# Opening of a scan-and-gate kernel: a bank for each turned tile, three groups for the first tokens, warming products on a cleared tile and in the gaps

## The chip, the cores and the metric

The kernel runs on one core of one Trainium2 chip. A core has five engines that run on their own and wait for each other by semaphores: TensorE (PE, matrix products; PEld is its weight load), VectorE (DVE), ScalarE (ACT), GpSimd (POOL) and SyncE (SP, which here issues nearly all DMAs). Products are summed in PSUM, which has eight banks; DVE and ACT read them out. The metric is the device time of one launch in microseconds (us); the median of some runs counts.

## What is computed

Tokens x (2048 of 448 numbers, bf16) are normalized, and then go two ways: through a diagonal complex recurrence (A) and through a gated product of three matrices (B). The results are multiplied.

```python
xn = _layernorm(x)
# A: Bu = xn @ B_bar.T;  h[t] = Lam_bar * h[t-1] + Bu[t];  s = 2 * real(h @ C.T) + xn * Dskip
s = _A_ref(xn, ...)
# B: g = xn @ w_gate (448 x 1792); u = xn @ w_up; h = sigmoid(g) * u; h @ w_down (1792 x 448)
g = silu(_B_ref(xn, ...))
return x + s * g
```

## The kernel before

**Tiling.** The 2048 tokens are cut into four chunks of 512 (TC), a chunk into four tiles of 128 tokens. Features of xn lie on partitions after a turn (transposition), as four blocks of 128 (KT = 4, the middle ones overlapping so that 64 rows of w_gate and 64 of w_up, the "tails", share one weight tile wt). The 1792 columns of w_gate and w_up are 14 groups of 128 (ft). A group has a gate sum g_ps and an up sum u_ps, each 128 x 512 in fp32, which is one bank each. One sum takes three whole products (128 rows) and one tail (64 rows).

**Order.** The order on every engine is the written order: `keep_order` at the end ties each instruction to the one before it on its engine. So a waiting instruction holds up all behind it on its engine.

**The opening (chunk 0, lines 928 to 1026)** differs from the rest. Input tiles come one by one; weights for groups 0 to 3 (512 columns) come behind them on SP's queue, then those for groups 4 to 9. PE first runs `warm(22)`: 128 x 128 products of the identity tile `ident`, which POOL builds with a memset and an affine select (L136, L137), into a bank that nobody reads. Then `turn_twice` turns the three vectors log_dt, Lambda_im, Lambda_re (tile `rows`), and `warm(5)` follows. For the first two tiles DVE takes the statistics (`ln_stats`, L214 and L215), ACT the inverse deviation (`ln_inv`, L249 and L250), DVE normalizes (`ln_norm`, L272), PE turns the tile with four 128 x 128 products (`ln_turn`, L286) into the PSUM tile `tps`, and DVE copies it out to xnT (`ln_out`, L289). For the third tile the sums come from ACT, for the fourth from DVE, and POOL takes the power (L244). A `warm(4)` stands behind the first two turns.

`tps` is one tile of one bank with a place for an even and an odd token tile (`tps[:, j % 2, ...]`). A copy out of it and a turn into it are therefore kept apart: each pair of copies stands behind both turns.

**Groups of the first tokens.** With the first two tiles (256 tokens, HC) in xnT, PE starts groups 0 to 3: `gu_wholes` (L713) runs whole products of a group's gate (which = 0) or up sum (1) over a stretch of tokens; `gu_half` (L706) runs a tail. The order is: gate 0, 1, 2, 3; up 0, 1; third turn; up 2; fourth turn; tails of groups 0 to 2 for the first and then the second 256 tokens; tails of group 3; then whole products of groups 0 to 2 over the second 256 tokens, and group 3's rest. All sums are complete only then, and `gu_out` (ACT, tanh, L719) and `up_copy` (DVE, L999) empty them. Between these, `emit_frac` and `emit_abs` (DVE, L429 and L435) and `emit_sin` and `emit_cos` (ACT, L440 and L443) build the angle tables of the recurrence.

**Behind the opening** two sums run side by side on the upper and lower 64 rows of PE (`beside_each`, products at L514), from group 4 on: `group` emits pairs of units (gate and up of a group, or `bu`, the input of the recurrence, whose weights bT come by DMA transposes at L294). A bank is free for a new sum when ACT or DVE has emptied its old one. ACT empties them with sigmoid and copy (L752).

**Banks.** All PSUM tiles share one tag with eight places. In the opening these are warm_ps, tp_v (the vectors), tps and the eight of four groups (`gus`), so that some groups take a bank over from warm_ps, tp_v or tps.

Of the kernel before, what the change touches and what calls it, by code (L numbers as in the profile page):

```python
# [11 lines left out]
BF16 = mybir.dt.bfloat16  # L12
# [5 lines left out]
D = 448  # L18
F = 1792
P = 128  # L20
TC = 512
HC = TC // 2
NCH = S_TOK // TC
TPC = TC // P
KT = 4
# [6 lines left out]
K_ROWS = (0, 128, 192, 320)  # L32
# [19 lines left out]
def two_runs(ap: bass.AP, step: int, n: int) -> bass.AP:  # L52
    return bass.AP(tensor=ap.tensor, offset=ap.offset, ap=[*ap.ap[:-1], [step, 2], [1, n]])
# [18 lines left out]
def kernel(  # L72
# [18 lines left out]
    pe, act, dve, pool, sync = nc.tensor, nc.scalar, nc.vector, nc.gpsimd, nc.sync  # L91
    w = ctx.enter_context(tc.tile_pool(name="w", bufs=1))
# [5 lines left out]
    ps = ctx.enter_context(tc.tile_pool(name="ps", bufs=2, space=bass.MemoryType.PSUM))  # L98
# [9 lines left out]
    xnT = [w.tile([P, KT, TC], BF16, name=f"xnT{c}") for c in range(3)]  # L108
# [10 lines left out]
    ident = w.tile([P, P], BF16, name="ident")  # L119
# [53 lines left out]
        sync.dma_start_transpose(out=ctr[nm][:, :, kt * CP:(kt + 1) * CP], in_=raw[nm][0:CP, kt, :])  # L173


    hpi = w.tile([P, 1], FP32, name="hpi")
    dve.memset(hpi[:], HALF_PI)
    sgn = w.tile([P, 1], FP32, name="sgn")
# [14 lines left out]

    warm_ps = ps.tile([P, P], FP32, name="warm_ps", tag="bank", bufs=8)

    def warm(n):
        for _ in range(n):
            pe.matmul(warm_ps[:], lhsT=ident[:], rhs=ident[:], start=True, stop=True)  # L198

    def turn_twice(o, src, n):  # L200

        for kt in range(3):
            pe.transpose(o[:, kt, 0:n], src[:, kt * P:(kt + 1) * P], ident[0:n, 0:n])
        pe.transpose(o[:, 3, 0:n], src[:, D - P:D], ident[0:n, 0:n])
        pe.transpose(o[0:64, 3, 0:n], src[:, 384:D], ident[0:n, 0:n])
# [10 lines left out]


    sums = w.tile([P, NT, 2], FP32, name="sums")

    junk = w.tile([P, D], BF16, name="junk")  # L220

    def ln_sum(t):
        c, j = divmod(t, TPC)
# [40 lines left out]
    def ln_norm(c, j):  # L264
        t = c * TPC + j
        xb, src = xn[c % 3][:, j, :], x_t[c][:, j, :]
        if c == 0:
            xb = xb[:, 0:D]
        else:
            xb, src = two_runs(xb, 2 * P, 2 * P), two_runs(src, 192, 2 * P)  # L270
        if c < 2:
            dve.tensor_scalar(out=xb, in0=src, scalar1=mv[:, t, 0:1], scalar2=rsd[:, t, :], op0=ALU.subtract,  # L272
                              op1=ALU.mult)
        else:
            act.activation(xb, src, ACT.Identity, bias=nmr[:, t, :], scale=rsd[:, t, :])
# [4 lines left out]
    def ln_turn(c, j):  # L280
        xb, cols = xn[c % 3], slice(j * P, (j + 1) * P)
        if c > 0:
            sync.dma_start_transpose(out=xnT[c][:, 0:KT, cols], in_=xb[:, j, :])
            return
        for kt in range(KT):
            pe.transpose(tps[:, j % 2, kt, :], xb[:, j, K_ROWS[kt]:K_ROWS[kt] + P], ident[:])  # L286

    def ln_out(j):
        dve.tensor_copy(out=xnT[0][:, :, j * P:(j + 1) * P], in_=tps[:, j % 2, :, :])  # L289

# [40 lines left out]
    def emit_steps():  # L333
        kq, nf, anf = col("kq", 2 * KT), col("nf", 2 * KT), col("anf", 2 * KT)
        tu = col("tu", 2 * KT)
        pool.tensor_copy(out=tu[:, 0:KT], in_=K["turn"][:])
        pool.tensor_single_scalar(out=tu[:, KT:2 * KT], in_=K["theta"][:], scalar=float(TC) / TWO_PI, op=ALU.mult)
        pool.tensor_single_scalar(out=kq[:], in_=tu[:], scalar=MAGIC, op=ALU.add)
        pool.tensor_single_scalar(out=kq[:], in_=kq[:], scalar=-MAGIC, op=ALU.add)
        pool.tensor_tensor(out=nf[:], in0=kq[:], in1=tu[:], op=ALU.subtract)  # L340
        K.update(nf=nf, anf=anf)
# [85 lines left out]
    def emit_frac(pt):  # L427
        f = sp.tile([P, HC], FP32, name="frac", tag="wv")
        dve.scalar_tensor_tensor(out=f[:], in0=iota_f[:], scalar=K["turn"][:, pt:pt + 1], in1=K[pt][:],  # L429
                                 op0=ALU.mult, op1=ALU.subtract)  # L430
        K[pt] = f

    def emit_abs(pt):
        af = sp.tile([P, HC], FP32, name="afrac", tag="td")
        dve.tensor_single_scalar(out=af[:].bitcast(I32), in_=K[pt][:].bitcast(I32), scalar=0x7FFFFFFF,  # L435
                                 op=ALU.bitwise_and)
        K[pt, 1] = af
# [62 lines left out]
    def bank(name, n=TC):  # L500
        return ps.tile([P, n], FP32, name=name, tag="bank", bufs=8)
# [27 lines left out]
    class Unit:  # L529

        ft = None
# [172 lines left out]
    def gu_half(c, ft, i, t, first, n0, n1):  # L704
        p0, kt = ((0, 1), (64, 2))[i]
        pe.matmul(t[:, n0:n1], lhsT=wt[p0:p0 + 64, ft * P:(ft + 1) * P], rhs=xnT[c][p0:p0 + 64, kt, n0:n1],  # L706
                  start=first, stop=not first)

    def gu_wholes(c, ft, gt, ut, first, n0=0, n1=TC, which=(0, 1)):
        f0, f1 = ft * P, (ft + 1) * P  # L710
        for t, wm, kts in [((gt, wg, GATE_K), (ut, wu, UP_K))[i] for i in which]:
            for k, kt in enumerate(kts):
                pe.matmul(t[:, n0:n1], lhsT=wm[:, k, f0:f1], rhs=xnT[c][:, kt, n0:n1],  # L713
                          start=(first and k == 0), stop=(not first and k == 2))
# [194 lines left out]
    def ln_plan(c):  # L909
        own, t0, n = c - 1, c * TPC, 2 if c == 2 else 0  # L910
        for k in range(n):
            at(0, 11 + k, 0.8, lambda t=t0 + k: ln_stats(t))
        t1, m = t0 + n, TPC - n
        steps = [lambda t=t: ln_sum(t) for t in range(t1, t1 + m)] + [lambda: ln_mean(t1, m)]
        steps += [lambda t=t: ln_square(t) for t in range(t1, t1 + m)]
        for k, f in enumerate(steps):
            at(own - 1, (10, 10, 11, 11, 12)[k] if c == 2 else "out%d" % min(k // 2, 3), 0.0, f)
        if n:
            at(0, 12, 0.17, lambda: ln_var(t0, n))
        then = (0, 13) if c == 2 else (own, 1)  # L920
        at(*then, 0.17, lambda: ln_var(t1, m, True))
        at(*then, 0.17, lambda: ln_minus(c))
        at(own, "down0", 0.0, lambda: (ln_pow(t0, TPC), ln_scale(c)))
        for j in range(TPC):
            at(own, "down0", 0.0, lambda j=j: ln_norm(c, j))
        at(own, "down0", 0.0, lambda: [ln_turn(c, j) for j in range(TPC)])

    dummy = w.tile([P, 1], FP32, name="dummy")
    act.add_instruction(mybir.InstLoadActFuncSet(name=nc.get_next_instruction_name(), act_func_set_id=LN_AND_EXP,
                                                 ins=[], outs=[]))  # L930
    warm(22)
    turn_twice(tp_v, rows, 3)
    tps = ps.tile([P, 2, KT, P], BF16, name="tp_x", tag="bank", bufs=8)
    gus = [(bank("g_ps"), bank("u_ps")) for _ in range(4)]
    warm(5)

    ln_stats(0)
# [6 lines left out]
    ln_sum(2)  # L944
    ln_norm(0, 0)
    ln_turn(0, 0)
    ln_norm(0, 1)
    ln_turn(0, 1)
    warm(4)
    ln_out(0)  # L950
    ln_out(1)
    ln_mean(2, 1)
    ln_square(2)
# [5 lines left out]
    act.activation(K["r"][:], K["arg"][:], ACT.Exp)  # L959
    act.activation(dummy[:], hpi[:], ACT.Silu)  # L960

    for ft in range(4):
        gu_wholes(0, ft, *gus[ft], True, 0, HC, (0,))
    for ft in range(2):
        gu_wholes(0, ft, *gus[ft], True, 0, HC, (1,))
    ln_norm(0, 2)
    ln_turn(0, 2)
    emit_frac(0)
    gu_wholes(0, 2, *gus[2], True, 0, HC, (1,))
    ln_norm(0, 3)  # L970
    ln_turn(0, 3)
    ln_out(2)
    emit_abs(0)
    ln_out(3)
    for pt in (1, 3, 2):
        emit_frac(pt)
        emit_abs(pt)
    for n0 in (0, HC):
        for ft in range(3):
            for i in range(2):  # L980
                gu_half(0, ft, i, gus[ft][i], n0 > 0, n0, n0 + HC)
    gu_half(0, 3, 0, gus[3][0], False, 0, HC)
    gu_half(0, 3, 1, gus[3][1], True, 0, TC)
    gu_half(0, 3, 0, gus[3][0], True, HC, TC)
    for ft in range(3):
        gu_wholes(0, ft, *gus[ft], False, HC, TC)
    gu_wholes(0, 3, *gus[3], False, HC, TC, (0,))
    gu_wholes(0, 3, *gus[3], False, 0, TC, (1,))
    emit_steps()
    emit_den()  # L990
    for pt in (0, 1, 3):
# [176 lines left out]
```

## Time and profile before

| | us |
|---|---|
| Times of the runs shown | 183.1, 183.21, 185.1 |
| Median | 183.21 |
| Profiled execution, time | 184.86 |
| Profiled execution, span (first to last instruction) | 183.1 |
| PE busy | 177.4 (97% of the span) |
| DVE busy | 163.0 (89%) |
| ACT busy | 115.2 (63%) |
| POOL busy | 23.5 (13%) |

The profile is one execution. Its page gives busy times by engine, the span in 40 slices, the chain of work that ended last, and groups of instructions; further views give waits, and instructions in order of time. In a timeline row stand the start and the length in us, the engine, the line of the kernel, the operation, what it writes and reads, how many were merged, and in brackets the idle time before it with what ended it. Matmuls overlap in a pipeline: a product's row is longer than the distance to the next one's start, and the distance is what it costs.

### The profile page before, as it was taken

Reading aid. Unit: us, or ns where it says so; the run is one execution under the profiler, and the core shown is the slowest. Engines: PE = TensorE matmul, PEld = TensorE weight load, DVE = VectorE, ACT = ScalarE, POOL = GpSimd, SP = SyncE. Lnnn points to the kernel's source line nnn. Section 1 sums busy time; section 2 is a strip of 40 time slices with the busy share of each in tenths; the row PEclk is TensorE's granted clock in tenths of the full one; section 3 lists DMA queues with packets and bytes.
Section 4 is the critical chain, followed back from the end, with each engine's and each line's share of the span. In section 5 each row is a group of like instructions: output and inputs, shape, how many; then the busy total and the mean of one; then the engine's idle time right before and its main releaser. Section 6 shows DMA issues by size and latency. Waiting matters only on the chain.

```text
span 183.1 us, 4318 instructions
## 1 busy us (share of the span) xinstructions
PE 177.4 (97%) x1633; PEld 89.0 (49%) x1633; DVE 163.0 (89%) x331; ACT 115.2 (63%) x238; POOL 23.5 (13%) x56
## 2 busy tenths in 40 slices
PE   7889999999999999999999999999999999999993
PEld 6665444444554444544554444544554444545552
DVE  4649969999999979999999999599999999499993
ACT  4959868997757896996647767146227676244100
POOL 3630765802000000006000000000000000000000
PEclk9999999999999999999999999999999999999999
DMA  5899964994344103111250002011000100011002
GB/s 155 250 303 165 250 169 66 306 273 103 79 82 86 29 4 100 29 55 52 59 61 0 0 13 48 4 50 50 4 15 15 32 0 2 4 50 52 0 30 74
DMA packets 26348, 14.27 MB, mean 78 GB/s; under 512 B 16083, under 2 KB 26070, under 8 KB 26326
## 3 DMA queue, kind: packets, MB, share of 16 engines
q1 hardware_dynamic: 26320, 13.98, 31.0%
q8 instruction: 13, 0.21, 0.5%
q14 instruction: 9, 0.07, 0.2%
q10 hardware_dynamic: 6, 0.00, 0.0%
HBM read 7.69 MB, written 1.84 MB: 52 GB/s over the span
## 4 chain that ended last, share of the span: by engine, by line
PE 95%; DVE 2%; ACT 0%; issue 0%; POOL 0%; POOLq 0%; DVEq 0%
PE g_ps L514 24%; PE u_ps L514 18%; PE d_ps L514 17%; PE bu L514 12%; PE y_ps L514 11%; PE d_ps L1111 6%; PE g_ps L713 2%; PE u_ps L713 2%; PE warm_ps L198 1%; DVE xnT L289 1%; PE tp_x L286 1%; DVE sg L860 0%; DVE o_l L866 0%; PE g_ps L706 0%; DVE xn L272 0%
## 5 line engine op out<-in xcount | busy, mean ns | idle before, releaser
L514 PE MATMUL u_ps<-xnT,wu 64*128 64x512 bf16 x312 | 61.4, 376 | 0.0
L514 PE MATMUL g_ps<-xnT,wg 64*128 64x512 bf16 x312 | 53.4, 376 | 0.0
L752 ACT ACTIVATE sig<-g_ps 128x512 bf16<-128x512 f32 x52 | 29.2, 597 | 29.1 <-PE g_ps L514 28.5
L514 PE MATMUL bu<-xnT,bT 64*128 64x512 bf16 x168 | 37.4, 376 | 0.0
L514 PE MATMUL d_ps<-wd,hF 64*128 64x448 bf16 x336 | 32.3, 349 | 0.0
L514 PEld LDWEIGHTS <-wu 64*128 64x128 bf16 x312 | 22.4, 94 | 18.5
L752 ACT CAST ub<-u_ps 128x512 bf16<-128x512 f32 x52 | 29.3, 606 | 0.6 <-DVE hF L723 0.4
L514 PEld LDWEIGHTS <-wg 64*128 64x128 bf16 x312 | 18.9, 94 | 18.3 <-issue 0.4
L514 PEld LDWEIGHTS <-hF 64*128 64x128 bf16 x336 | 16.4, 94 | 15.6
L611 DVE TENSOR_TENSOR_SCAN wv<-r_col,st,ta 128x512 bf16<-128x512 f32 x18 | 22.7, 1278 | 0.2
L514 PE MATMUL y_ps<-ct,h 64*128 64x448 bf16 (+2 forms) x203 | 22.1, 343 | 0.0
L749 DVE TENSOR_TENSOR hF<-sig,ub 128x512 bf16<-128x512 bf16 x52 | 21.1, 415 | 0.4 <-ACT ub L752 0.3
L514 PEld LDWEIGHTS <-bT 64*128 64x128 bf16 x168 | 15.8, 94 | 10.0
L514 PE MATMUL g_ps<-xnT,wt 64*128 64x512 bf16 x52 | 19.6, 376 | 0.0
L514 PE MATMUL u_ps<-xnT,wt 64*128 64x512 bf16 x52 | 19.6, 376 | 0.0
L514 PEld LDWEIGHTS <-h 64*128 64x128 bf16 (+1 forms) x203 | 11.6, 95 | 9.9
L592 ACT CAST bus<-bu 128x512 bf16<-128x512 f32 x24 | 14.3, 597 | 2.1 <-PE bu L514 2.1
L776 ACT ACTIVATE sigd<-d_ps 128x448 bf16<-128x448 f32 x12 | 6.6, 553 | 14.1 <-PE d_ps L514 14.1
L514 PEld LDWEIGHTS <-wt 64*128 64x128 bf16 x104 | 9.8, 94 | 6.2
L244 POOL TENSOR_TENSOR rsd<-ve,mhalf 128x1 f32<-128x1 f32 (+2 forms) x6 | 6.3, 1052 | 45.5 <-PE bu L514 45.4
L831 DVE TENSOR_TENSOR o_t<-y_ps,xn 128x448 bf16<-128x448 f32 x12 | 6.9, 618 | 4.8 <-PE y_ps L514 4.8
L1111 PE MATMUL d_ps<-wd,hF 128*128 128x448 bf16 x56 | 10.9, 353 | 0.0
(151 smaller groups left out, 239.6 us busy)
## 6 DMA issues: line engine op xcount, KB each, us to landing
wd<-in_B_w_down_dram SPq DMA_DIRECT2D x1, 1568.0 KB, 7.7
x<-in_A_x_dram SPq DMA_DIRECT2D x3, 448.0 KB, 4.7
out_dram<-o_t SPq DMA_DIRECT2D x6, 224.0 KB, 2.1
wg<-in_B_w_gate_dram SPq DMA_DIRECT2D x2, 256.0 KB, 3.4
wu<-in_B_w_up_dram SPq DMA_DIRECT2D x2, 256.0 KB, 4.2
bsw<-bus SPq DMA_DIRECT2D x4, 128.0 KB, 2.8
wsw<-wv SPq DMA_DIRECT2D x8, 64.0 KB, 1.9
c_re<-in_A_C_re_dram SPq DMA_DIRECT2D x1, 392.0 KB
```

The source lines that it names most:

```text
L198: pe.matmul(warm_ps[:], lhsT=ident[:], rhs=ident[:], start=True, stop=True)
L244: pool.tensor_tensor(out=rsd[:, t:t + n, :], in0=ve[:, t:t + n, :], in1=mhalf[:, 0:n, :], op=ALU.pow)
L286: pe.transpose(tps[:, j % 2, kt, :], xb[:, j, K_ROWS[kt]:K_ROWS[kt] + P], ident[:])
L514: m = pe.matmul(self.t[:, n0:n1], lhsT=lhsT, rhs=rhs, start=self.done == 1, stop=self.done == self.n)
L592: empty = [lambda cc=cc: act.copy(out=bus[:, cc, :], in_=pst[cc][:]) for cc in range(2)]
L611: dve.tensor_tensor_scan(out=T["wv"][:, cc, :], data0=rb, data1=T["ta"][:, cc, :], initial=(0.0 if c == 0 else st[pt][:, cc, :]), op0=mul, ...
L713: pe.matmul(t[:, n0:n1], lhsT=wm[:, k, f0:f1], rhs=xnT[c][:, kt, n0:n1], start=(first and k == 0), stop=(not first and k == 2))
L749: dve.tensor_tensor(out=h[:], in0=sig[:], in1=ub[:], op=ALU.mult)
L752: u.empty = [lambda: act.activation(sig[:], gt[:], ACT.Sigmoid), lambda: act.copy(out=ub[:], in_=ut[:])]
L776: act.activation(sigd[:], ds[j][:], ACT.Sigmoid)
L831: dve.tensor_tensor(out=two_runs(o[:, i, :], HD, HD), in0=two_runs(ys[c, j + 2 * i][:], HD, HD), in1=xn_runs(c, j + 2 * i), op=ALU.add)
L1111: pe.matmul(ds[j][:], lhsT=hF[c, ft][:, j * P:(j + 1) * P], rhs=wd[:, ft, :], start=ft == 0, stop=ft == FT - 1)
```

## The change

Seven edits, all in the opening:

- The tile `junk` (a place for results that nobody reads) is made earlier, and DVE clears its first 128 columns as its first instruction. `warm` takes a tile; the first warming products run on `junk` in place of `ident`, 26 in place of 22.
- `tps` becomes two tiles with a bank each, one for even and one for odd token tiles. `ln_turn` and `ln_out` take them by `j % 2`.
- Two warming products stand between the first two turns, and six in place of four behind the second.
- Only three groups get banks at first (`gus` of three). Whole products of the first 256 tokens: gate 0, 1, 2; up 0, 1; third turn; up 2; fourth turn.
- The fourth group gets its two banks after the last copy. Its tails and whole products run over all 512 tokens, the whole products behind those of groups 0 to 2.
- On DVE, `emit_frac(0)` stands ahead of the third normalization in place of behind it, and `emit_abs(0)` ahead of the fourth in place of between the two copies.
- PE has four pairs of weight load and product more in all: eight warming products more, and four fewer of the fourth group (its gate sum was made in two halves).

```diff
--- before.py
+++ after.py
@@ -173,6 +173,8 @@
         sync.dma_start_transpose(out=ctr[nm][:, :, kt * CP:(kt + 1) * CP], in_=raw[nm][0:CP, kt, :])
 
 
+    junk = w.tile([P, D], BF16, name="junk")
+    dve.memset(junk[:, 0:P], 0.0)
     hpi = w.tile([P, 1], FP32, name="hpi")
     dve.memset(hpi[:], HALF_PI)
     sgn = w.tile([P, 1], FP32, name="sgn")
@@ -193,9 +195,9 @@
 
     warm_ps = ps.tile([P, P], FP32, name="warm_ps", tag="bank", bufs=8)
 
-    def warm(n):
+    def warm(n, t=ident):
         for _ in range(n):
-            pe.matmul(warm_ps[:], lhsT=ident[:], rhs=ident[:], start=True, stop=True)
+            pe.matmul(warm_ps[:], lhsT=t[:, 0:P], rhs=t[:, 0:P], start=True, stop=True)
 
     def turn_twice(o, src, n):
 
@@ -216,8 +218,6 @@
 
 
     sums = w.tile([P, NT, 2], FP32, name="sums")
-
-    junk = w.tile([P, D], BF16, name="junk")
 
     def ln_sum(t):
         c, j = divmod(t, TPC)
@@ -283,10 +283,10 @@
             sync.dma_start_transpose(out=xnT[c][:, 0:KT, cols], in_=xb[:, j, :])
             return
         for kt in range(KT):
-            pe.transpose(tps[:, j % 2, kt, :], xb[:, j, K_ROWS[kt]:K_ROWS[kt] + P], ident[:])
+            pe.transpose(tps[j % 2][:, kt, :], xb[:, j, K_ROWS[kt]:K_ROWS[kt] + P], ident[:])
 
     def ln_out(j):
-        dve.tensor_copy(out=xnT[0][:, :, j * P:(j + 1) * P], in_=tps[:, j % 2, :, :])
+        dve.tensor_copy(out=xnT[0][:, :, j * P:(j + 1) * P], in_=tps[j % 2][:])
 
 
 
@@ -928,10 +928,10 @@
     dummy = w.tile([P, 1], FP32, name="dummy")
     act.add_instruction(mybir.InstLoadActFuncSet(name=nc.get_next_instruction_name(), act_func_set_id=LN_AND_EXP,
                                                  ins=[], outs=[]))
-    warm(22)
+    warm(26, junk)
     turn_twice(tp_v, rows, 3)
-    tps = ps.tile([P, 2, KT, P], BF16, name="tp_x", tag="bank", bufs=8)
-    gus = [(bank("g_ps"), bank("u_ps")) for _ in range(4)]
+    tps = [ps.tile([P, KT, P], BF16, name="tp_x", tag="bank", bufs=8) for _ in range(2)]
+    gus = [(bank("g_ps"), bank("u_ps")) for _ in range(3)]
     warm(5)
 
     ln_stats(0)
@@ -944,9 +944,10 @@
     ln_sum(2)
     ln_norm(0, 0)
     ln_turn(0, 0)
+    warm(2)
     ln_norm(0, 1)
     ln_turn(0, 1)
-    warm(4)
+    warm(6)
     ln_out(0)
     ln_out(1)
     ln_mean(2, 1)
@@ -959,33 +960,30 @@
     act.activation(K["r"][:], K["arg"][:], ACT.Exp)
     act.activation(dummy[:], hpi[:], ACT.Silu)
 
-    for ft in range(4):
-        gu_wholes(0, ft, *gus[ft], True, 0, HC, (0,))
-    for ft in range(2):
-        gu_wholes(0, ft, *gus[ft], True, 0, HC, (1,))
+    for i in range(2):
+        for ft in range(3 - i):
+            gu_wholes(0, ft, *gus[ft], True, 0, HC, (i,))
+    emit_frac(0)
     ln_norm(0, 2)
     ln_turn(0, 2)
-    emit_frac(0)
+    emit_abs(0)
     gu_wholes(0, 2, *gus[2], True, 0, HC, (1,))
     ln_norm(0, 3)
     ln_turn(0, 3)
     ln_out(2)
-    emit_abs(0)
     ln_out(3)
     for pt in (1, 3, 2):
         emit_frac(pt)
         emit_abs(pt)
+    gus.append((bank("g_ps"), bank("u_ps")))
     for n0 in (0, HC):
         for ft in range(3):
             for i in range(2):
                 gu_half(0, ft, i, gus[ft][i], n0 > 0, n0, n0 + HC)
-    gu_half(0, 3, 0, gus[3][0], False, 0, HC)
-    gu_half(0, 3, 1, gus[3][1], True, 0, TC)
-    gu_half(0, 3, 0, gus[3][0], True, HC, TC)
-    for ft in range(3):
-        gu_wholes(0, ft, *gus[ft], False, HC, TC)
-    gu_wholes(0, 3, *gus[3], False, HC, TC, (0,))
-    gu_wholes(0, 3, *gus[3], False, 0, TC, (1,))
+    for i in range(2):
+        gu_half(0, 3, i, gus[3][i], True, 0, TC)
+    for ft in range(4):
+        gu_wholes(0, ft, *gus[ft], False, (0 if ft == 3 else HC), TC)
     emit_steps()
     emit_den()
     for pt in (0, 1, 3):
```

## The prediction

> **What bounds the kernel now.** I read the page's busy times and its chain, then the waits of the opening, then the timeline of the first 22 us.
>
> ```profile
> PE 177.4 (97%) x1633; PEld 89.0 (49%) x1633; DVE 163.0 (89%) x331; ACT 115.2 (63%) x238; POOL 23.5 (13%) x56
> ...
> PE 95%; DVE 2%; ACT 0%; issue 0%; POOL 0%; POOLq 0%; DVEq 0%
> ```
>
> ```profile
> PE g_ps L706 <- DVE xnT L289: 0.6, 1, 0.6
> ...
> PE g_ps L713 <- DVE xnT L289: 0.4, 1, 0.4
> ```
>
> TensorE (PE) carries 95% of the chain, so a microsecond taken out of PE's opening is a microsecond off the end, as long as nothing behind it is late. The waits name two holes on PE: 0.4 us before the first gate product and 0.6 us before the first tail of the second 256 tokens. Both are waits for VectorE's (DVE's) copies of turned tiles.
>
> A third loss is not in the waits. It is the rate of the products:
>
> ```profile
> 1.34 2.53 PE L198 MATMUL warm_ps<-ident 128*128 128x128 bf16 x22 [1.34 <-POOL ident L137]
> ...
> 3.81 0.23 PE L203 MATMUL tp_v<-ident,rows 3*128 3x3 bf16 x3
> ...
> 4.14 0.71 PE L198 MATMUL warm_ps<-ident 128*128 128x128 bf16 x5
> ...
> 5.40 0.34 PEld L286 LDWEIGHTS <-xn 128*128 128x128 bf16 x4 [0.37 <-DVE xn L272]
> ...
> 5.80 0.63 PE L198 MATMUL warm_ps<-ident 128*128 128x128 bf16 x4
> ...
> 6.86 2.72 PE L713 MATMUL g_ps<-xnT,wg 128*128 128x256 bf16 x12 [0.42 <-DVE xnT L289]
> ...
> 9.37 1.26 PE L713 MATMUL u_ps<-xnT,wu 128*128 128x256 bf16 x6
> ...
> 9.80 0.83 PE L713 MATMUL u_ps<-xnT,wu 128*128 128x256 bf16 x4
> ...
> 10.46 0.39 PE L286 MATMUL tp_x<-ident,xn 128*128 128x128 bf16 x4
> ...
> 10.69 0.49 PE L713 MATMUL u_ps<-xnT,wu 128*128 128x256 bf16 x3
> ...
> 11.01 0.39 PE L286 MATMUL tp_x<-ident,xn 128*128 128x128 bf16 x4
> ```
>
> ```profile
> 6.84:10.26 3.42, 3.40 (x17) 1.00 0.84 240
> ```
>
> Starts are the measure, since ends are modelled. Twelve 256-column products start between 6.86 and 9.37: 0.209 each (0.213 without the first). Three start between 10.69 and 11.01: 0.109 each. The four from 9.80 to 10.46 took 0.66, so two ran at 0.213 and two at 0.109: PE doubled its rate near 10.25, after 3.4 us of unbroken work. The 22 warming products before (about 0.107 each for 128 columns, 1.34 to 3.7; at full rate four turns start from 10.46 to 10.69, 0.057 each) did not bring it, nor did the broken stretch 4.14 to 6.23. The third number of the last row, the granted clock, says 1.00 for 6.84 to 10.26 and does not show this; the spacing decides.
>
> [...]
>
> [...] The shown times are 183.1, 183.21 and 185.1, and the profiled execution took 184.86 (its span 183.1 and 1.76 around it): two levels 1.8 apart. Test it: with full rate from 6.86 on, 18 products take 1.96 (to 8.82), the third turn 0.22, three products 0.33, and the fourth turn starts at 9.37 in place of 11.01: 1.64 earlier, and 184.86 - 1.64 = 183.22. That is the median shown. So I take the profiled execution for a late one (release at 10.25) and the median for an early one (release before 6.86).
>
> **Part by part.** The rows for the opening's other engines:
>
> ```profile
> 0.79 0.06 DVE L177 MEMSET hpi<- 128x1 f32 x1 [0.79 <-PEq L1152]
> ...
> 3.13 0.94 SPq L134 DMA_DIRECT2D wu<-in_B_w_up_dram  x2
> ...
> 4.95 0.40 DVE L272 TENSOR_SCALAR xn<-x,mv,rsd 128x448 bf16<-128x448 bf16 x1 [0.32 <-ACT rsd L250]
> ...
> 6.05 0.76 DVE L289 COPY xnT<-tp_x 128x512 bf16<-128x512 bf16 x2 [0.70 <-PE tp_x L286]
> ...
> 6.51 1.69 ACT L424 ACTIVATE whole<-iota_f,turn 128x256 int32<-128x256 f32 x4
> ...
> 6.72 0.62 DVE L214 BATCH_NORM_STATS2 stats<-x 128x6 f32<-128x448 bf16 x1
> ...
> 7.58 0.40 DVE L272 TENSOR_SCALAR xn<-x,mv,rsd 128x448 bf16<-128x448 bf16 x1
> ...
> 7.66 1.10 SPq L134 DMA_DIRECT2D wu<-in_B_w_up_dram  x2
> ...
> 7.88 0.50 DVE L429 SCALAR_TENSOR_TENSOR frac<-iota_f,turn,whole 128x256 f32<-128x256 f32 x1
> ...
> 7.92 0.56 POOL L244 TENSOR_TENSOR rsd<-ve,mhalf 128x1 f32<-128x1 f32 x1
> ...
> 8.51 0.40 DVE L272 TENSOR_SCALAR xn<-x,mv,rsd 128x448 bf16<-128x448 bf16 x1
> ...
> 11.44 0.42 DVE L289 COPY xnT<-tp_x 128x512 bf16<-128x512 bf16 x1 [2.53 <-PE tp_x L286]
> ...
> 11.78 0.28 DVE L435 TENSOR_SCALAR afrac<-frac 128x256 int32<-128x256 int32 x1
> ...
> 11.98 0.42 DVE L289 COPY xnT<-tp_x 128x512 bf16<-128x512 bf16 x1
> ...
> 12.45 0.27 PE L706 MATMUL g_ps<-xnT,wt 64*128 64x256 bf16 x1 [0.62 <-DVE xnT L289]
> ...
> 15.40 0.81 PE L713 MATMUL u_ps<-xnT,wu 128*128 128x512 bf16 x3
> ...
> 16.15 0.82 PE L514 MATMUL g_ps<-xnT,wg 64*128 64x512 bf16 x6
> ```
>
> ```profile
> wu<-in_B_w_up_dram SPq DMA_DIRECT2D x1, 192.0 KB, 5.2
> ...
> wu<-in_B_w_up_dram SPq DMA_DIRECT2D x1, 128.0 KB, 4.1
> ```
>
> *Cleared tile.* One DVE memset goes first. It is not in the trace; the nearest rows are its neighbours at 0.06, which I take, and the far bound is a normalization's 0.40. DVE starts at 0.79, so I let PE start at 0.9 rather than 1.34. 26 products at 0.107 end at 3.68, before 3.81, where the row vectors' turns start anyway, so the four more products are hidden. Were the memset 0.40, they would end at 4.02 and 0.2 us would come through, since ScalarE's queue copies those vectors (L316) ahead of the second tile's scale (L250).
>
> *Gaps filled.* Products now stand at 0.9 to 3.68, 4.14 to 5.31 (two more, 0.21 between the turns, where PE stood idle to 5.40) and on to 5.80 plus six, 6.44. In the 3.4 us before 6.84 PE idles about 0.6 us (0.12, the vectors' turns 0.33, 0.1, 0.05) where it idled about 1.4 (0.14, 0.33, 0.04, 0.31 and 6.23 to 6.86). [...]
>
> *Own banks.* The first copy no longer waits for the second turn. DVE's second normalization ends at 5.35; the first copy runs 5.38 to 5.76, the second starts at 6.05 as before at half rate (turn at 5.40 plus 0.65), 5.84 at full rate. Copies end 6.43 or 6.22 instead of 6.81: the first gate product starts at 6.48, 0.38 earlier. The six warming products ahead of it end at 6.44 at the worst, so they hide; each further one would cost 0.107.
>
> *Three groups first.* PE then has 9 gate and 6 up products, not 12 and 6: 6.48 + 15 x 0.109 = 8.12. The last of the first up weights, second of the two issues from 3.13, starts at 3.6 and lands 4.1 later, 7.7; the four products behind it make 8.2. The third tile: statistics start at 6.47 (0.25 earlier), 0.86 to the next instruction as before, 7.33; the fraction, now ahead (its input is the first of four ScalarE results from 6.51, ready by 6.95), 0.50, 7.85; normalization 0.40, 8.25: 0.27 later than before. Third turn 8.30 to 8.52, products 0.33 to 8.85. Fourth: the absolute value 0.28 and normalization 0.40 end at 8.97; GpSimd's power (7.92 + 0.56 = 8.48) is ready. Fourth turn at 9.02; the third tile's copy meanwhile, to 9.40; the fourth copy from 9.45 (turn to copy 0.43, as 11.01 to 11.44) to 9.87; first tail of the second half at 9.91, where before it stood at 12.45.
>
> *Fourth group at the end.* From that tail to the first line-514 product before takes 16.15 - 12.45 = 3.70. The fourth group's tails cost 0.22 instead of 0.33; its gate products cover 512 columns, three at 0.216 (the three from 15.40 take 0.75 to 16.15, 0.1 of it the change of line) in place of three at 0.109, 0.32 more. So 3.91: PE is at the line-514 work at 13.82, 2.33 earlier than in the profiled execution.
>
> *Behind it.* The rest of every queue keeps its order. Three things could be late. The up weights of group 4 are issued second from 7.66, about 8.3, and land 5.2 later, 13.5; they are needed 0.86 behind 13.82. The others:
>
> ```profile
> L294 SPq DMA_TRANSPOSE bT<-in_A_B_im_dram x2: 1292/1437/1582, 14.4 to 15.7; - x2
> ...
> DMA to landing us min/median/max: 4.3/4.6/6.3
> ```
>
> ```profile
> 19.97 1.08 ACT L752 CAST ub<-u_ps 128x512 bf16<-128x512 f32 x2
> ...
> 22.20 0.38 PE L514 MATMUL bu<-xnT,bT 64*128 64x512 bf16 x1
> ```
>
> The second imaginary half of bT is issued at 15.7 and lands 4.6 later, 20.3; its first product comes 0.86 (four products of 0.216) behind 22.20 - 2.33, 20.73: 0.4 to spare. ScalarE's copy of the fifth group's up sum (ended 21.05) frees the bank needed 0.65 behind 19.87, at 20.52. ScalarE's chain before it hangs on the angle tables, which hang on DVE behind the fourth copy (12.40, now 9.87) and on ScalarE's own table load, and so moves by about 1.5: 19.5. If it moved by nothing, 0.5 us would be lost.
>
> **Sum.** 184.86 - 2.33 = 182.53, and against the median's early execution 183.22 - 182.53 = 0.7 gained. Own range 182.1 to 183.0 (0.5 for ScalarE or the memset; 0.2 below if copies and turns run at full rate).
>
> **Rivals.**
> *A, forecast:* early release in most executions, 182.5. For it: the test above. Against: no trace shows an early one.
> [...]
> [...]
> *D, the profile is typical:* its 1.65 over the median is only the profiler's cost, and unprofiled executions are late. Then the same 2.33 come off the median: 180.88. Against it: three unprofiled times differ by 2.0 among themselves.
>
> **Numbers.** A 0.65, B 0.17, D 0.10, C 0.05, the rest (a bank or copy that I placed wrongly) 0.03. The time is A's, 182.5. The range takes A and B, with 0.3 under A's own bounds and 0.15 over B: 181.8 to 184.2; C and D stay out. About 1%, 1.8 us, is what a measurement of this kernel can tell from no change: faster means under 181.38 (D and a little of A), 0.13; slower over 185.04 (C and half the rest), 0.06; same 0.81. A's own sign is faster, by 0.4%.
>
> **What would show it.** Early release: gate products 0.109 apart from the first. Own banks: first copy near 5.4, first gate product near 6.3 to 6.5. Third turn near 8.3, fourth near 9.0, first tail of the second half near 9.9, line 514 near 13.8. Half-rate spacing to 10.2 means B, to 13 means C. A bu product later than 19.9, with PE waiting on a transfer or on ScalarE, would break the part behind the opening.

## The result, and the profile after

| | before | after |
|---|---|---|
| Median of 20 runs each | 184.09 | 182.79 |
| Lowest and highest | 183.1 to 185.36 | 182.65 to 183.93 |
| Profiled execution, time | 184.86 | 182.77 |
| Profiled execution, span | 183.1 | 181.0 |

The ratio after to before is 0.9931, 95% interval 0.9905 to 0.9957: 0.7% faster, inside the 1% that was called no change. The forecast was 182.5, the range 181.8 to 184.2.

The 20 times of before fall in two groups with nothing between: ten from 183.1 to 183.44 and ten from 184.74 to 185.36. Its median, 184.09, is a time that no execution took, and moves with the number of runs in each group. All 88 executions of before that were timed in this study keep to the two groups (38 up to 183.5, 50 from 184.4). After has one group: 19 of 20 runs between 182.65 and 183.21, and one at 183.93. So the change does two things: it takes the upper group away, and its median is 0.46 under that of the lower one (183.25).

The timeline of after's opening, PE's and DVE's rows that answer to those shown of before (start and length in us, engine, line, operation, what it writes and reads, how many, idle time before):

```profile
0.80 0.11 DVE L177 MEMSET junk<- 128x64 uint32 x1 [0.80 <-PEq L1150]
...
0.97 2.96 PE L200 MATMUL warm_ps<-junk 128*128 128x128 bf16 x26 [0.97 <-DVE junk L177]
...
3.86 0.23 PE L205 MATMUL tp_v<-ident,rows 3*128 3x3 bf16 x3
...
4.19 0.71 PE L200 MATMUL warm_ps<-ident 128*128 128x128 bf16 x5
...
4.74 0.50 PE L286 MATMUL tp_x<-ident,xn 128*128 128x128 bf16 x4
...
5.07 0.28 PE L200 MATMUL warm_ps<-ident 128*128 128x128 bf16 x2
...
5.31 0.42 DVE L289 COPY xnT<-tp_x 128x512 bf16<-128x512 bf16 x1
...
5.45 0.40 PE L286 MATMUL tp_x<-ident,xn 128*128 128x128 bf16 x4
...
5.68 0.50 PE L200 MATMUL warm_ps<-ident 128*128 128x128 bf16 x6
...
5.88 0.42 DVE L289 COPY xnT<-tp_x 128x512 bf16<-128x512 bf16 x1 [0.16 <-PE tp_x L286]
...
6.23 0.62 DVE L216 BATCH_NORM_STATS2 stats<-x 128x6 f32<-128x448 bf16 x1
6.36 1.14 PE L713 MATMUL g_ps<-xnT,wg 128*128 128x256 bf16 x9 [0.18 <-DVE xnT L289]
...
7.46 0.91 PE L713 MATMUL u_ps<-xnT,wu 128*128 128x256 bf16 x6
7.63 0.40 DVE L272 TENSOR_SCALAR xn<-x,mv,rsd 128x448 bf16<-128x448 bf16 x1
...
7.94 0.28 DVE L435 TENSOR_SCALAR afrac<-frac 128x256 int32<-128x256 int32 x1
7.95 0.69 POOL L244 TENSOR_TENSOR rsd<-ve,mhalf 128x1 f32<-128x1 f32 x1
...
8.20 0.39 PE L286 MATMUL tp_x<-ident,xn 128*128 128x128 bf16 x4
...
8.42 0.49 PE L713 MATMUL u_ps<-xnT,wu 128*128 128x256 bf16 x3
...
8.68 0.40 DVE L272 TENSOR_SCALAR xn<-x,mv,rsd 128x448 bf16<-128x448 bf16 x1 [0.45 <-POOL rsd L244]
...
8.99 0.42 DVE L289 COPY xnT<-tp_x 128x512 bf16<-128x512 bf16 x1
...
9.13 0.40 PE L286 MATMUL tp_x<-ident,xn 128*128 128x128 bf16 x4 [0.21 <-DVE xn L272]
...
9.56 0.42 DVE L289 COPY xnT<-tp_x 128x512 bf16<-128x512 bf16 x1 [0.16 <-PE tp_x L286]
...
10.04 0.27 PE L706 MATMUL g_ps<-xnT,wt 64*128 64x256 bf16 x1
...
10.37 0.38 PE L706 MATMUL g_ps<-xnT,wt 64*128 64x512 bf16 x1
...
10.69 0.50 PE L713 MATMUL g_ps<-xnT,wg 128*128 128x256 bf16 x3
```

Read the rates first. The five warming products from 4.19 stand 0.107 apart, the six from 5.68 only 0.056 (the last starts at 5.96), and the nine gate products from 6.36 stand 0.109 apart from the first one on, where before's stood 0.213 apart to 10.2. Then the copies: the first (L289) starts at 5.31, while the second turn has not begun. Then what is late next: the fourth normalization (8.68) had been idle for GpSimd's power, and PE waited for it. The waits of the first 18 us say the same (who waited for what, us in all, times, the longest):

```profile
PEld L286 <- DVE xn L272: 0.8, 2, 0.5
...
DVE xn L272 <- POOL rsd L244: 0.5, 1, 0.5
...
PEld L713 <- DMA wu<-in_B_w_up_dram: 0.4, 2, 0.2
...
DVE xnT L289 <- PE tp_x L286: 0.3, 2, 0.2
```

The copies' wait for turns is 0.3 us in all. New on the list are the waits for the up weights and for GpSimd. The work behind the opening, at line 514, starts at 14.06, where before's profiled execution had it at 16.15:

```profile
13.32 0.81 PE L713 MATMUL u_ps<-xnT,wu 128*128 128x512 bf16 x3
...
14.06 0.61 PE L514 MATMUL g_ps<-xnT,wg 64*128 64x512 bf16 x4
...
20.11 0.38 PE L514 MATMUL bu<-xnT,bT 64*128 64x512 bf16 x1
```

2.09 earlier here, and 184.86 - 182.77 = 2.09 at the end: nothing of it was lost behind the opening. The input of the recurrence (`bu`) starts at 20.11, without a wait.

### The profile page after: what moved, and what is told of

Its sections match the earlier page's. It is cut to its first block, busy times and chain, and to the rows that moved or that the text cites. A ratio compares the mean times of both kernels' runs of the same rounds, so it can differ in the third digit from the quotient of the medians.

```text
span 181.0 us, 4324 instructions
## 1 busy us (share of the span) xinstructions
PE 176.2 (97%) x1636; PEld 87.8 (49%) x1637; DVE 163.2 (90%) x332; ACT 114.9 (63%) x238; POOL 24.8 (14%) x56
## 4 chain that ended last, share of the span: by engine, by line
PE 94%; POOL 1%; DVE 1%; issue 1%; ACT 0%; DVEq 0%; POOLq 0%
PE g_ps L514 25%; PE u_ps L514 19%; PE d_ps L514 18%; PE bu L514 12%; PE y_ps L514 11%; PE d_ps L1109 6%; PE warm_ps L200 2%; PE g_ps L713 1%; PE u_ps L713 1%; POOL rsd L244 1%; DVE sg L860 0%; PE g_ps L706 0%; DVE o_l L866 0%; DVE xnT L289 0%; PE tp_x L286 0%
## 5 line engine op out<-in xcount | busy, mean ns | idle before, releaser
L244 POOL TENSOR_TENSOR rsd<-ve,mhalf 128x1 f32<-128x1 f32 (+2 forms) x6 | 5.8, 961 | 44.1 <-PE bu L514 43.9
```

Source lines behind the costliest of these rows:

```text
L244: pool.tensor_tensor(out=rsd[:, t:t + n, :], in0=ve[:, t:t + n, :], in1=mhalf[:, 0:n, :], op=ALU.pow)
```

## The experiments

The median of each kernel is over 10 to 12 executions. Its ratio is to the kernel before on the same chip, whose median there was 184.70 (experiments 1 to 4) or 184.77 (5 to 8). The ratio lies close to that of the mean times, so it depends on how many executions of before fell into the upper group; the groups themselves say more. An execution is called early or late by the group of its time. "Released" means that PE's rate doubled (in before's trace from one 256-column product in 0.213 us to one in 0.109), and the release theory of the expectations is that the two groups differ in when it does.

**1. The warming edits alone.** The kernel before, with this (the lines that matter; `warm` takes a tile, as in the change):

```diff
+    junk = w.tile([P, D], BF16, name="junk")
+    dve.memset(junk[:, 0:P], 0.0)
-    warm(22)
+    warm(26, junk)
     ln_turn(0, 0)
+    warm(2)
     ln_norm(0, 1)
     ln_turn(0, 1)
-    warm(4)
+    warm(6)
```

> The kernel before with the warming edits alone (26 products on the cleared tile, two more between the first turns, six behind the second). [...] Rival (the new banks and order make the difference, the warming is idle work): two levels as before, 183.2 and 185.1.

Measured: median 183.20, all 12 runs from 183.01 to 183.28; ratio to before 0.9949 (0.9917 to 0.9982). The upper group is gone, the lower one stands where it was. The warming takes the late executions away and gives an early one nothing. Its profiled execution is an early one with before's order and one bank, which no trace of before had shown:

```profile
6.86 1.47 PE L713 MATMUL g_ps<-xnT,wg 128*128 128x256 bf16 x12 [0.51 <-DVE xnT L289]
...
10.81 0.27 PE L706 MATMUL g_ps<-xnT,wt 64*128 64x256 bf16 x1 [0.61 <-DVE xnT L289]
```

**2. Everything but the warming.** The changed kernel, with before's warming:

```diff
-    warm(26, junk)
+    warm(22)
-    warm(2)
-    warm(6)
+    warm(4)
```

> The changed kernel with the warming of before (22 products on the identity, none between the turns, four behind). Release theory: two levels, about half the executions each, early ones at 182.7 to 182.9 and late ones near 184.0 (1.2 to 1.3 apart, less than before's 1.85 since three fewer products are early). Rival: one level at 182.8.

Measured: nine runs from 182.74 to 183.05 and three from 184.09 to 184.43; median 182.86, ratio 0.9952 (0.9913 to 0.9992). Two groups again, some 1.4 apart, close to the two places forecast (the upper one 0.1 to 0.4 above its own); three late of twelve rather than half, which so few runs do not tell from half.

**3. One bank for both turned tiles.** The changed kernel, with `tps` of before (turns and copies index it as before):

```diff
-    tps = [ps.tile([P, KT, P], BF16, name="tp_x", tag="bank", bufs=8) for _ in range(2)]
+    tps = ps.tile([P, 2, KT, P], BF16, name="tp_x", tag="bank", bufs=8)
```

> The changed kernel with one bank for both turned tiles again. If the copies' wait for the second turn is on the path: the third copy starts behind the fourth turn (about 9.55 instead of 9.0), the fourth copy ends near 10.4 instead of 9.98, 0.4 later, 183.1 to 183.2, one level. The later first copies (gate start 6.7 instead of 6.36) cost nothing by themselves, as PE waits for up weights to 7.75 and for GpSimd's power to 9.1 anyway. Rival (hidden): 182.8.

Measured: median 183.23, eleven runs from 183.12 to 183.59 and one at 184.72; ratio 0.9959 (0.9925 to 0.9992). The timeline of this kernel:

```profile
6.70 1.14 PE L713 MATMUL g_ps<-xnT,wg 128*128 128x256 bf16 x9 [0.51 <-DVE xnT L289]
...
8.33 0.39 PE L286 MATMUL tp_x<-ident,xn 128*128 128x128 bf16 x4
...
9.18 0.40 PE L286 MATMUL tp_x<-ident,xn 128*128 128x128 bf16 x4
...
9.62 0.76 DVE L289 COPY xnT<-tp_x 128x512 bf16<-128x512 bf16 x2 [0.49 <-PE tp_x L286]
...
10.42 0.27 PE L706 MATMUL g_ps<-xnT,wt 64*128 64x256 bf16 x1 [0.41 <-DVE xnT L289]
```

The third copy waits for the fourth turn (9.62 instead of 8.99) and the first tail of the second half stands at 10.42 instead of 10.04. The gate products start 0.34 later than in the changed kernel, but the third turn only 0.13 later and the fourth 0.05. So the own banks bring all of the 0.44 us that the change gains on an early execution, and they bring it at the second pair of copies, not at the first. With one bank the three early groups and the new order bring nothing (183.23 against 183.20 of experiment 1). The first tail of the second half does stand 0.39 earlier than in experiment 1 (10.42 against 10.81), but from it to line 514 the new order takes 4.02 (10.04 to 14.06 in the changed kernel's trace) in place of before's 3.70 (12.45 to 16.15), as the fourth group's gate products now all come behind it. By the count of banks, eight places of one tag in the kernel, three early groups are what makes room for the second bank; no run has four groups and two banks. The one execution at 184.72 was not expected, and no trace shows it.

**4. The fourth tile's inverse on ScalarE.** The changed kernel, with this (and `lnv` of four columns in place of two):

```diff
-    ln_pow_of(3, 1, mv[:, 3:4, 1:2], 1.0)
-    for pt in (0, 1, 3, 2):
+    emit_whole(0)
+    ln_inv(3)
+    for pt in (1, 3, 2):
         emit_whole(pt)
```

> The changed kernel with the fourth tile's inverse deviation taken by ScalarE (logarithm and exponential, as for the first two) behind the first of the four whole-turn tiles, in place of GpSimd's power. In the changed kernel's trace the fourth normalization waits 0.45 us for GpSimd's power (8.64) and PE waits for it from 8.75 to 9.13. Theory (GpSimd is what is late next): fourth turn at about 8.75, first tail of the second half near 9.66 instead of 10.04, 0.35 less: 182.3 to 182.5. Rival (ScalarE's table chain, 0.5 later by it, becomes the bound): 182.8 or more.

Measured: median 182.43, ten runs from 182.28 to 182.60; ratio to before 0.9898 (0.9864 to 0.9933).

```profile
7.62 0.40 DVE L272 TENSOR_SCALAR xn<-x,mv,rsd 128x448 bf16<-128x448 bf16 x1
...
8.13 0.39 DVE L272 TENSOR_SCALAR xn<-x,mv,rsd 128x448 bf16<-128x448 bf16 x1
...
8.76 0.39 PE L286 MATMUL tp_x<-ident,xn 128*128 128x128 bf16 x4
...
9.66 0.27 PE L706 MATMUL g_ps<-xnT,wt 64*128 64x256 bf16 x1
```

The fourth normalization starts at 8.13 instead of 8.68, the fourth turn follows the up products without a gap, the first tail stands at 9.66: 0.38 earlier, and the median is 0.36 lower than the changed kernel's. GpSimd's power was what was late next. Part of that is its queue: in the changed kernel GpSimd takes the third tile's power from 7.01 to 7.59 and starts on the fourth's numbers at 7.67, where ScalarE here starts at 7.31. This version's median lies under both kernels'.

**5. The early start alone.** The kernel before, with the cleared tile and `warm(26, junk)`, no products in the gaps.

> The kernel before with one warming edit, the 26 products on the cleared tile (start near 0.97 instead of 1.34), no products in the gaps. [...] Release theory: mostly the early level 183.0 to 183.4, late executions near 185 left in about one of six. Rival (the start alone is what counts, an unbroken 2.7 us): none late. Rival (it does nothing): half late.

Measured: nine runs from 183.01 to 183.31 and three from 184.77 to 185.16; median 183.22, ratio 0.9975 (0.9936 to 1.0014). Late executions remain, so the early start alone is not what counts. Three of twelve is no difference from one in six, a figure that was the author's estimate and that no run shows; but experiment 2, with none of the new warming, had three of twelve late too, so these runs do not show that the early start alone helps.

**6. The gap products alone.** The kernel before, with `warm(2)` and `warm(6)`, and the 22 products on the identity.

> The kernel before with the gap products alone (two more between the first turns, six behind the second), start at 1.34 with 22 products on the identity. [...] Release theory: no execution near 185, most at 183.0 to 183.4, a few up to 183.6. Rival (the early start is what counts): half late.

Measured: eleven runs from 183.05 to 183.59 and one at 185.42; median 183.23, ratio 0.9959 (0.9922 to 0.9997). The two at 183.51 and 183.59 lie inside the forecast; no trace shows what they were. The one at 185.42 does not fit: none near 185 was expected, and no trace shows it either. With one bank the gate products of this kernel start at 6.81, behind 0.51 us in which PE had nothing, and not at 6.48, as the prediction worked out for the changed kernel; whether that gap has to do with the late execution is open. The profiled execution is an early one, like experiment 1's:

```profile
6.81 1.47 PE L713 MATMUL g_ps<-xnT,wg 128*128 128x256 bf16 x12 [0.51 <-DVE xnT L289]
...
9.32 0.39 PE L286 MATMUL tp_x<-ident,xn 128*128 128x128 bf16 x4
...
10.76 0.27 PE L706 MATMUL g_ps<-xnT,wt 64*128 64x256 bf16 x1 [0.62 <-DVE xnT L289]
...
14.46 0.82 PE L514 MATMUL g_ps<-xnT,wg 64*128 64x512 bf16 x6
```

**7. Warming with turns.** The changed kernel, with every warming product made a transposition, 22 at the start (and `warm_ps` in bf16):

```diff
-            pe.matmul(warm_ps[:], lhsT=t[:, 0:P], rhs=t[:, 0:P], start=True, stop=True)
+            pe.transpose(warm_ps[:], t[:, 0:P], ident[:])
-    warm(26, junk)
+    warm(22)
```

> The changed kernel with every warming product made a turn (transposition of the identity or of the same tile, same count of columns), 22 at the start, on the identity. If turns count as work for the clock as products do: as the changed kernel, 182.7 to 183.2, turn spacing 0.107 going to 0.056 before 6.9. [...]

Measured: all 12 runs from 182.64 to 182.90, median 182.80; ratio 0.9913 (0.9884 to 0.9943).

```profile
4.14 0.71 PE L200 MATMUL warm_ps<-ident 128*128 128x128 bf16 x5
...
5.89 0.84 PE L200 MATMUL warm_ps<-ident 128*128 128x128 bf16 x6
...
6.61 1.51 PE L713 MATMUL g_ps<-xnT,wg 128*128 128x256 bf16 x9
...
7.95 0.82 PE L713 MATMUL u_ps<-xnT,wu 128*128 128x256 bf16 x6
...
8.61 0.39 PE L286 MATMUL tp_x<-ident,xn 128*128 128x128 bf16 x4
```

From 6.61 to 7.95 nine gate products start, 0.149 apart in the mean: four at 0.213 and five at 0.109 make 1.40, so the rate doubled near 7.4. Real products had then run for 0.8 us; in before's profiled execution, warmed by products, they ran for 3.4 us (6.86 to 10.25) before it doubled. Warming with turns alone left none of twelve executions late: they lie from 182.64 to 182.90, the changed kernel's 20 from 182.65 to 183.93, and the late ones of experiment 2 from 184.09 to 184.43. Whether a turn does as much for the release as a product, and by what rule, no run shows. This execution also shows that a release as late as 7.4 costs nothing in the changed kernel: its third turn stands at 8.61 in place of 8.20, but its up products are through at 9.16, when the fourth tile's normalization, which waits for GpSimd, has just ended too (8.71 to 9.11).

**8. The fourth turn ahead of the up products.** Experiment 4, with this:

```diff
+    ln_norm(0, 3)
+    ln_turn(0, 3)
     gu_wholes(0, 2, *gus[2], True, 0, HC, (1,))
-    ln_norm(0, 3)
-    ln_turn(0, 3)
```

> The changed kernel with the fourth tile's inverse on ScalarE (as in the run before) and the fourth turn ahead of the third group's up products. With ScalarE's inverse the fourth tile is normalized by 8.53, and PE runs the up products to 8.75 first. Theory: fourth turn at 8.55, the last copy then hangs on the copy before it (ends 9.05), ends 9.47 instead of 9.61, first tail of the second half near 9.5 instead of 9.66: 0.13 to 0.15 less, 182.25 to 182.35. Rival (DVE's two copies were the bound already): 182.43 as without it.

Measured: 182.47, runs from 182.22 to 183.48; ratio 0.9906 (0.9874 to 0.9938). No gain over 182.43: the median misses what the theory forecast.

```profile
8.92 0.94 DVE L289 COPY xnT<-tp_x 128x512 bf16<-128x512 bf16 x2
...
9.23 0.49 PE L713 MATMUL u_ps<-xnT,wu 128*128 128x256 bf16 x3
...
9.65 0.28 PE L706 MATMUL g_ps<-xnT,wt 64*128 64x256 bf16 x1
...
9.99 0.27 PE L706 MATMUL g_ps<-xnT,wt 64*128 64x256 bf16 x1
```

The last copy ends at 9.86, but PE is busy with its own queue to then: the up products moved behind the turn push the first half's tails to 9.65, and the second half's follow at 9.99 without a gap. So in this execution it is neither the turn nor the copies that the second half waits for, as theory and rival had it, but PE's own work behind the fourth normalization. How much the order is worth stays open: this profiled execution took 182.79, 0.3 over the median, and its second token tile came 0.4 late (the second statistics start at 3.97, in experiment 4 at 3.59). Counted from the third normalization (8.04 here, 7.62 there), the first tail of the second half stands 0.09 earlier than in experiment 4, a gain too small for runs that spread over 0.6 us.

## Why the prediction was right

**Two levels.** The prediction took before's profiled execution (184.86) for one with a late release, and worked out an early one: first tail of the second half at 12.45 - 1.64 = 10.81, line 514 at 16.15 - 1.64 = 14.51, time 183.22. Experiment 1 caught such an execution: tail at 10.81, time 183.22. Experiment 6's has the tail at 10.76, line 514 at 14.46 and a time of 183.24, and the lower group of before lies from 183.1 to 183.44. This step, which rested on three times and one trace, carried the forecast: with the profile taken as typical (rival D, 180.88) it would have been 2 us off. The range alone would not have told much, since it reached to 184.2 and took in before's own median of 184.09; the rates and the starts in the trace do.

**Early release.** The sum takes the products at 0.109 from the first gate product on. How much work, or of what kind, has to stand ahead of them for that, no run shows; that most executions would be released early was the author's estimate. In after's profiled execution the rate doubles between 4.93 and 5.02, in the first turn. Of the other executions there are only times: 19 of 20 lie within 0.5 us of its own, but by experiment 7 a release up to 7.4 would give the same time. Other profiled executions were released at quite different moments:

- experiment 2's ahead of its first turn at 5.02 (four turns in 0.40, where experiment 1's first four, not yet released, take 0.63);
- experiment 6's near 5.8, where the distance of its warming products goes from 0.107 to 0.056;
- experiment 1's near 5.9, experiment 4's near 6.5, experiment 7's near 7.4;
- before's near 10.25.

What sets the moment, and why nothing lies between the two groups of before, no run shows.

**Rivals B and C** stood for half-rate spacing to 10.2 and to 13. No run shows the terms on which these two and their chances (0.17 and 0.05) rest. What the runs show in their place: in after's trace the gate products stand 0.109 apart from the first one, and experiment 7, with every warming product a turn of `pe.transpose`, has no late execution (182.64 to 182.90). The highest run of after is 183.93. What that one was is open, as are those at 184.72 in experiment 3 and 185.42 in experiment 6.

**The gain on an early execution was over-sized:** 0.7 forecast, 0.46 measured (182.79 against a lower group around 183.25). Line 514 was placed at 13.82 and stands at 14.06. Two terms make up the 0.24:

- *The fourth normalization.* It was put at 8.57 to 8.97 with GpSimd's power "ready" at 8.48. The power ran 7.95 to 8.64 (0.69; the 0.56 was before's), and the normalization 8.68 to 9.08. The longer power goes with the change itself: it took 0.56 in the three traces with before's order on DVE (before and experiments 1 and 6), where the fraction runs beside it, and 0.69 to 0.74 in the four with the new order (after and experiments 2, 3, 7), where the absolute value does (7.94 in after). Why, no run shows. The first tail came at 10.04 and not 9.91: 0.13. The list of things that could be late left GpSimd out, and experiment 4 shows that it was the first of them.
- *The fourth group's tails.* They were put at 0.22 for 512 columns against 0.33 for before's halves. From the pair's start at 10.37 to the next gate product at 10.69 it is 0.33, the same as before's from 12.78 to 13.10: 0.11.

**Two places where the steps were off and it did not matter.** The cleared tile's memset took 0.11 and not 0.06, and PE started at 0.97 and not 0.9; the 26 products still ended ahead of the vectors (3.86). The third normalization was put 0.27 later than before, and came 0.05 later (7.63), because the earlier copies let the statistics start at 6.23. PE was not ready for it anyway: the up weights held it, 0.4 us in two waits, to 7.75, as forecast (7.7).

**Behind the opening** nothing was late, as forecast: 2.09 at line 514 is 2.09 at the end.

## What to carry to other kernels

Where a kernel's times fall in two groups, find out which one the profile shows before pricing a change against the median, and read PE's rate from the distance of starts in the first 10 us, not from the clock column, which says 1.00 for 6.84 to 10.26 of before, with products 0.213 apart. Filling PE's gaps before the first real product with idle products did not make an execution faster than the lower group here (183.01 to 183.28 in experiment 1), it made that group the rule: both kinds together left none of twelve executions late, the gap products alone one, the early start alone three, against 50 of 88 without; that the early start is needed, so few do not show. And when a wait is taken away, look at every engine that feeds the same instruction for what is late next: here it was a 0.7 us power on GpSimd, and moving it gave 0.36 us, nearly as much again as the banks.

## What was not expected of the hardware

Of before's executions 50 of 88 took some 1.8 us, 1% of the kernel, longer than the rest; in the profiled one, where the warming stops 0.6 us short of the first product (6.23 to 6.86) and PE idles 1.4 us of the 3.4 ahead of it, PE's rate doubled only near 10.25. Warming with transpositions alone left none of twelve executions late (182.64 to 182.90). And the GpSimd power of one column took 0.56 us with one DVE instruction beside it and 0.69 to 0.74 with another, while ScalarE's logarithm and exponential, 0.29 and 0.20 in before's trace and in experiment 4's, did the same in 0.49.
